# Silu as a tanh in one token chunk, the ends of the paired layers reordered, the first keys loaded in two pieces, and due times shifted from kept random seeds

## The chip, the cores and the metric

The kernel runs on one core of a Trainium2 chip. The metric is device time in microseconds of one execution. A core has a matrix engine (TensorE, PE in the profile, with PEld for its weight loads), a vector engine (VectorE, DVE), an engine for activation functions (ScalarE, ACT), GpSimd (POOL) and SyncE (SP), which issues nearly all DMAs here. Matrix products end in PSUM, of which the kernel uses eight banks of 128 x 512 fp32 numbers; all else lies in SBUF.

## The reference

```python
def phi(x):                        # x: 4 batches x 8 heads x 576 tokens x 64
    proj = einsum('bhsd,md->bhsm', x, omega)            # 128 features
    h = proj - sum(x * x, -1) / 2
    return exp(h - max(h, -1)) / sqrt(m)
q_p, k_p = phi(q * scale), phi(k * scale)
kv, z = k_p^T v, sum(k_p over tokens)
x = (q_p kv) / (q_p z + 1e-6)      # -> 2304 tokens x 512
g = x @ w_gate; x = (g * sigmoid(g) * (x @ w_val)) @ w_out     # 512 -> 1536 -> 512
out = ((x @ w_a) * (x @ w_b)) @ w_out2                          # 512 -> 1536 -> 512
```

## The kernel before

The 2304 tokens are cut into five chunks (`spans`): 512, 512, 256, 512 and 512 columns, features on the partitions. The first three go through attention and two feed-forward layers by `layer(c, m)`, with c the chunk and m = 0 for the layer with silu, 1 for the second. In it, each of 12 blocks `f` takes two PSUM banks, one for the gate and one for the value, of 4 x 3 products each (every fp32 product is made of three in fp32r: high x high, high x low, low x high; ACT makes the high part by a copy, DVE the low part by a subtraction, `wh`/`wl` for weights, `hh`/`hl` for the block's result). ACT applies Silu to the gate bank into `a` (L954), DVE multiplies it by the value bank into `h` (L957). A bank is free again when its last reader has ended. The last two chunks of 512 go together, by `pair(m)`, which makes 2 x 2 blocks in seven products in place of eight (`seven`, products p1 to p7 of mixed operands a11, s1 to s4, t1 to t4 and so on, each of 6 matmuls). `mixes` makes the activations' mixed operands ahead of a layer, `blocks` those of the inner result, `up` runs the first half, `down` and `plain` the second. `snap` copies a bank by ACT at its first use, `plus` adds one by DVE.

Attention of later chunks runs beside the layers of earlier ones. It needs Exp on ACT (L632), whose table set is another than that of Silu: between the two stands an ACT_TABLE_LOAD, which the compiler puts in.

The order of the instructions on each engine is made by a planner, `Plan`, when the program is built. Each step is recorded with its engine, an estimated duration, what it reads and writes, and a due time; `Plan.order` replays the steps on five engines and takes on each, whenever it comes free, the ready step with the earliest due time. It also deals out the buffers of each ring (PSUM banks among them) in that replay. The result is a fixed order for each engine. At run time an engine takes its instructions strictly in that order.

```python
on(ACT, act(n, 0, True), due, lambda a=a, ps=ps: nc.scalar.activation(
    out=a.tile[:, 0:n], in_=ps[0].tile[:, 0:n], func=AF.Silu if m == 0 else AF.Copy),
    reads=[(ps[0],)], writes=[(a,)], table="silu" if m == 0 else None)
on(DVE, dve(n), due, lambda a=a, h=h, ps=ps: nc.vector.tensor_tensor(
    out=h.tile[:, 0:n], in0=a.tile[:, 0:n], in1=ps[1].tile[:, 0:n], op=ALU.mult),
    reads=[(a,), (ps[1],)], writes=[(h,)])
```

Of the kernel before, what the change touches and what calls it, by code (L numbers as in the profile page):

```python
# [12 lines left out]
AF = mybir.ActivationFunctionType  # L13
# [3 lines left out]
P = 128  # L17
# [79 lines left out]
class Plan:  # L97
# [14 lines left out]
    RATE = 0.24  # L112
    HELD = {DVE: (1.0, 0.05), POOL: (1.0, 0.12)}
# [4 lines left out]
    def add(self, eng, pace, due, fn, reads=(), writes=(), lat=None, table=None, size=0.0, slack=0.0,  # L118
# [22 lines left out]
        return o  # L141

# [121 lines left out]
    def issue(self):  # L264
        for o in self.order():
            o.fn()
# [3 lines left out]
def attention_moe_moe(ctx: ExitStack, tc: tile.TileContext, qT, kT, q, k, v, omegaT,  # L270
# [217 lines left out]
    AHEAD = 20.0  # L488

# [43 lines left out]
    def features(rT, tok, nt, step, f, due, length, how, psum, first):  # L533
# [39 lines left out]
        for g in range(0, nt, size):  # L573
# [25 lines left out]
            else:  # L599
                ps = psum.buf()  # L600
                for i in range(n):
                    def proj(i=i, ps=ps, g=g):
# [8 lines left out]
                    on(PE, pe(0.36 if how == SPLIT else 0.45), d, proj,  # L611
                       reads=[(hi,), (lo,), (bdh,), (bdl,)] if how == SPLIT else
                       [(rT, *rT.state), (bd, *bd.state)], writes=[(ps, i)])
# [24 lines left out]
    def loads(rT, src, p, due, pieces):  # L638

        for b, a, z, to in pieces:  # L640
            on(SP, dma((z - a) / 2), due - 9, lambda b=b, a=a, z=z, to=to: nc.sync.dma_start(
                out=rT.tile[:, to:to + z - a], in_=src[b, p][:, a:z]), writes=[(rT, b)])
# [3 lines left out]
    def keys(b, p, due, length, how):  # L646

        rT, tok, vt = r_xT.buf(), r_kt.buf(), r_vt.buf()
        loads(rT, kT, p, due, [(b, 0, S, 0)])
# [9 lines left out]
                 first=due < 4)  # L659
# [265 lines left out]
    def layer(c, m):  # L925
# [16 lines left out]
        for f in range(NF):  # L942
# [4 lines left out]
            for g in range(2):  # L947
# [6 lines left out]
            on(ACT, act(n, 0, True), due, lambda a=a, ps=ps: nc.scalar.activation(  # L954
                out=a.tile[:, 0:n], in_=ps[0].tile[:, 0:n], func=AF.Silu if m == 0 else AF.Copy),
                reads=[(ps[0],)], writes=[(a,)], table="silu" if m == 0 else None)
            on(DVE, dve(n), due, lambda a=a, h=h, ps=ps: nc.vector.tensor_tensor(  # L957
                out=h.tile[:, 0:n], in0=a.tile[:, 0:n], in1=ps[1].tile[:, 0:n], op=ALU.mult),
                reads=[(a,), (ps[1],)], writes=[(h,)])
# [59 lines left out]
    def mixes(m, due, eng):  # L1019
# [6 lines left out]
        def keep(name, k, b):  # L1026
# [61 lines left out]
    def pair(m, eng):  # L1088
# [23 lines left out]
        def seven(w, x, late, read):  # L1112


            b0, b1, b2 = (ps_m.buf() for _ in range(3))
            b4, b3 = (b2, b1) if late else (b1, b2)
# [5 lines left out]
            for i, name in enumerate(order):  # L1122
                b, wn, xn, first, last = steps[name]
                product(b, w[wn], x[xn], now(6 * i), first, last)
                read(name, b)

        def up(f, late):
# [18 lines left out]
            seven(w, x, late, read)  # L1146
# [9 lines left out]
        def down(g, d, hx):  # L1156

            w = mixed_weights(m, 2 * NF + ND * d + g, 2 * NF + ND * (d + KD // 2) + g, now(), d == 0)
            e = now(42) - 15
# [5 lines left out]
            seven(w, hx, d == 0, read)  # L1165

        def plain(g, d, hx, more):
# [4 lines left out]
            for t, names in ((1, ("a21", "a22")), (0, ("a11", "a12"))):  # L1172
                for x, o in zip(i, (d, d + KD // 2)):
                    b = ps_m.buf()
                    hi, lo = parts_of[c, m, x]
                    for k, name in enumerate(names):
                        product(b, [(hi, lo, slice((2 * k + e) * P, (2 * k + e + 1) * P))
                                    for e in range(2)], hx[name], now(more), k == 0, k == 1)
                        more += 6
                    gain(b, (t, o), now(more) - 15)  # L1180
# [43 lines left out]
        for f, out in steps:  # L1224
# [90 lines left out]
```

## Time and profile before

| | us |
|---|---|
| median of 3 runs | 1002.58 (1001.65 to 1002.89) |
| profiled execution, its own time | 1005.29 |
| its span, first to last instruction | 1003.5 |
| PE busy in the span | 984.2 (98%) |
| DVE busy | 894.3 (89%) |
| ACT busy | 725.3 (72%) |
| POOL busy | 258.2 (26%) |

The profiled execution is 1.8 us longer than its span and 2.7 us longer than the median of the runs without a profile. Times below are from the span's start. PE is busy nearly always, so time can only be had where it waits, where its clock is low, or before its first and after its last matmul. The first chunk's attention stands alone in the first 57 us; the layers of the three single chunks go on to about 650 us (the third chunk's first layer from 529 to 575 us), the paired layers from 650 us to the end, with the step from the first to the second paired layer at 824 us.

### The profile page before, as it was taken

The page shows a single profiled execution, that of the slowest core. Times are in us where ns is not written, and L with a number is a line of the kernel's source. Part 1 is how long each engine was busy: PE and PEld are TensorE (multiplying, and loading weights), DVE is VectorE, ACT ScalarE, POOL GpSimd, SP SyncE. Part 2 cuts the span into 40 slices and gives each one's busy share as a digit, 9 for nine tenths or more (in the row PEclk, how much of TensorE's full clock was granted, in tenths as well). Part 3 has the DMA queues.
Part 4 walks back from the last instruction along what each step waited for, and adds up shares of the span by engine and source line. Part 5 has one row for each costly group of instructions (what it writes and reads, how often), then busy time and mean ns, then how long its engine had stood idle before and what let it go on. Part 6 is the DMA issues. An engine that isn't in the chain of part 4 may idle for free.

```text
span 1003.5 us, 15362 instructions
## 1 busy us (share of the span) xinstructions
PE 984.2 (98%) x5144; PEld 829.3 (83%) x5144; DVE 894.3 (89%) x1593; ACT 725.3 (72%) x1523; POOL 258.2 (26%) x207
## 2 busy tenths in 40 slices
PE   7999999999999999999999999999999999999998
PEld 6878888878878888888888999988888887888886
DVE  5999889999968889998978879989889788989997
ACT  5978878798789898879868978666574645556351
POOL 1220023413502333454356424112020021202020
PEclk9999999999999999999999999999999999999999
DMA  8778776686876567665654555511212301121212
GB/s 250 238 258 243 229 244 200 217 252 189 286 227 197 176 190 241 203 188 166 192 165 131 147 160 172 171 61 33 74 43 63 95 22 53 32 74 42 61 35 84
DMA packets 92400, 153.12 MB, mean 153 GB/s; under 512 B 8736, under 2 KB 41120, under 8 KB 92320
## 3 DMA queue, kind: packets, MB, share of 16 engines
q1 hardware_dynamic: 92240, 152.11, 49.3%
q8 instruction: 40, 0.66, 0.3%
q14 instruction: 40, 0.33, 0.1%
q10 hardware_dynamic: 80, 0.03, 0.0%
HBM read 128.52 MB, written 23.59 MB: 152 GB/s over the span
## 4 chain that ended last, share of the span: by engine, by line
PE 78%; DVE 9%; ACT 6%; DMA 3%; issue 2%; POOL 1%; SPq 0%; DVEq 0%; ACTq 0%; POOLq 0%
PE ps_m L994 12%; PE ps_m L936 12%; PE ps_m L937 11%; PE ps_m L938 11%; PE ps_t L994 8%; PE ps_p L994 8%; PE ps_kv L994 4%; PE ps_kv L663 3%; PE ps_p L583 2%; DMA w64a<-w 1%; PE ps_t L869 1%; DVE wl L478 1%; PE ps_p L609 1%; PE ps_t L854 1%; DVE w L905 1%
## 5 line engine op out<-in xcount | busy, mean ns | idle before, releaser
L478 DVE TENSOR_TENSOR wl<-w,wh 128x512 fp32r<-128x512 f32 x254 | 190.8, 761 | 10.2 <-ACT wh L917 9.6
L936 PE MATMUL ps_m<-xh,wh 128*128 128x512 f32 (+1 forms) x504 | 189.2, 375 | 3.2 <-ACT a L954 2.5
L937 PE MATMUL ps_m<-xl,wh 128*128 128x512 f32 (+1 forms) x504 | 184.7, 366 | 0.7 <-DVE xl L478 0.7
L938 PE MATMUL ps_m<-xh,wl 128*128 128x512 f32 (+1 forms) x504 | 184.5, 366 | 0.7 <-DVE wl L478 0.7
L917 ACT ACTIVATE wh<-w 128x512 fp32r<-128x512 f32 x220 | 135.9, 632 | 32.1 <-DVE w L905 18.6
L478 POOL TENSOR_TENSOR rs<-xT,rs 64x576 fp32r<-64x576 f32 (+4 forms) x48 | 67.9, 1414 | 201.4 <-ACT rs L566 114.6
L936 PEld LDWEIGHTS ps_m<-xh,wh 128*128 128x128 f32 x504 | 95.9, 190 | 18.2 <-ACT a L954 3.8
L938 PEld LDWEIGHTS ps_m<-xh,wl 128*128 128x128 f32 x504 | 95.6, 190 | 16.8 <-DVE wl L478 1.2
L937 PEld LDWEIGHTS ps_m<-xl,wh 128*128 128x128 f32 x504 | 95.9, 190 | 13.7 <-DVE xl L478 1.3
L936 PE MATMUL ps_m<-hh,wh 128*128 128x512 f32 (+1 forms) x240 | 90.9, 379 | 0.0
L937 PE MATMUL ps_m<-hl,wh 128*128 128x512 f32 (+1 forms) x240 | 88.6, 369 | 0.0
L938 PE MATMUL ps_m<-hh,wl 128*128 128x512 f32 (+1 forms) x240 | 88.6, 369 | 0.0
L905 DVE SCALAR_TENSOR_TENSOR w<-w,w64a 128x512 uint32<-128x512 uint32 x90 | 69.9, 780 | 5.3 <-ACT w L896 5.2
L902 DVE SCALAR_TENSOR_TENSOR w64a<-w64a 128x512 uint32<-128x512 uint32 x90 | 69.0, 772 | 3.0 <-ACT w64a L899 2.9
L899 ACT ACTIVATE w64a<-w64a 128x512 uint32<-128x512 uint32 x90 | 60.9, 681 | 13.4 <-DMA w64a<-w 12.9
L896 ACT ACTIVATE w<-w64a 128x512 f32<-128x512 f32 x90 | 60.1, 675 | 0.6 <-DVE wl L478 0.6
L478 DVE TENSOR_TENSOR hl<-h,hh 128x512 fp32r<-128x512 f32 (+1 forms) x72 | 51.9, 722 | 1.6 <-ACT hh L960 1.4
L938 PEld LDWEIGHTS ps_m<-hh,wl 128*128 128x128 f32 x240 | 45.2, 189 | 8.0
L936 PEld LDWEIGHTS ps_m<-hh,wh 128*128 128x128 f32 x240 | 45.3, 189 | 7.6 <-issue 1.7
L960 ACT ACTIVATE hh<-h 128x512 fp32r<-128x512 f32 (+1 forms) x72 | 40.3, 561 | 15.3 <-DVE h L957 15.1
L937 PEld LDWEIGHTS ps_m<-hl,wh 128*128 128x128 f32 x240 | 45.4, 189 | 5.9
L825 POOL TENSOR_TENSOR xt<-qf,fT 128x512 f32<-128x512 f32 (+2 forms) x31 | 35.3, 1140 | 49.9 <-ACT qf L632 26.7
(850 smaller groups left out, 2635.4 us busy)
## 6 DMA issues: line engine op xcount, KB each, us to landing
w64a<-w SPq DMA_DIRECT2D x90, 512.0 KB, 4.3
w<-kept SPq DMA_DIRECT2D x180, 256.0 KB, 2.7
kept<-w SPq DMA_DIRECT2D x72, 256.0 KB, 5.0
w64b<-w SPq DMA_DIRECT2D x18, 512.0 KB, 4.7
kt<-k_t SPq DMA_DIRECT2D x16, 320.0 KB, 3.8
vt<-v_t SPq DMA_DIRECT2D x16, 320.0 KB, 4.4
xT<-kT SPq DMA_DIRECT2D x16, 288.0 KB, 3.8
qt<-q_t SPq DMA_DIRECT2D x16, 256.0 KB, 4.0
```

The source lines that it names most:

```text
L478: eng.tensor_tensor(out=out, in0=a, in1=hi.bitcast(F32), op=ALU.subtract)
L825: nc.gpsimd.tensor_tensor(out=pr.tile.rearrange("p (t h m) -> p t h m", t=2, h=2)[lo_:hi_, i:i + m], in0=f.tile[lo_:hi_, g + i:g + i + m], ...
L896: on(ACT, act(CW + 50), due - ahead - 10, lambda: nc.scalar.activation(out=w.tile, in_=raw.tile[:, :, 1].bitcast(F32), func=AF.Abs, scale= ...
L899: on(ACT, act(CW + 50), due - ahead - 10, lambda: nc.scalar.activation(out=raw.tile[:, :, 0], in_=raw.tile[:, :, 0], func=AF.Copy, scale=0 ...
L902: on(DVE, dve(CW, True), due - ahead - 9, lambda: nc.vector.scalar_tensor_tensor(out=raw.tile[:, :, 0], in0=raw.tile[:, :, 1], scalar=0x80 ...
L905: on(DVE, dve(CW, True), due - ahead - 9, lambda: nc.vector.scalar_tensor_tensor(out=w.tile.bitcast(U32), in0=w.tile.bitcast(U32), scalar= ...
L917: on(ACT, act(CW), due - ahead - 7, lambda: nc.scalar.activation(out=hi.tile.rearrange("p a c -> p (a c)"), in_=w.tile, func=AF.Copy), rea ...
L936: nc.tensor.matmul(o, lhsT=hi.tile[:, wi], rhs=a, start=first, stop=False)
L937: nc.tensor.matmul(o, lhsT=hi.tile[:, wi], rhs=b, start=False, stop=False)
L938: nc.tensor.matmul(o, lhsT=lo.tile[:, wi], rhs=a, start=False, stop=last)
L960: on(ACT, act(n), due + 2, lambda h=h, hh=hh: nc.scalar.activation(out=hh.tile[:, 0:n], in_=h.tile[:, 0:n], func=AF.Copy), reads=[(h,)], w ...
L994: nc.tensor.matmul(ps.tile, lhsT=flat(a.tile)[:, k], rhs=b.tile, start=first and i == j == 0, stop=last and i == len(w) - 1 and j == 2, sk ...
```

## The change

Six edits, all in one diff:

- In the third chunk only (`TANH = (2,)`), silu of the gate bank is made from tanh: ACT takes tanh(g/2) into `a`, DVE makes a = (a + 1) * g from the gate bank, and then h = 0.5 * a * value in place of a * value. The step no longer asks for Silu's table set.
- `Plan.shift` adds to the due times, before the order is made, the random shifts of 16 fixed seeds.
- The first keys' transposed load is cut into two DMAs of 240 and 336 columns, and a projection waits for those of them that it reads.
- `seven` takes its PSUM banks as its products come and can be run in turns with another; in the second paired layer the last two `down` blocks run interleaved, after the first two products of each.
- The last `plain` block of the first paired layer makes its four outputs in another order.
- In `mixes` the operands a11 and s3 are due 6 us earlier; the cold first projections are recorded with a longer duration.

```diff
+    KEPT = (400000, 400001, 400011, 400014, 400026, 400048, 400059, 400114, 400140, 400491,
...
+    def shift(self):
+        for k in self.KEPT:
+            rnd = random.Random(k)
+            size, share = (0.5, 1.0, 2.0)[k % 3], (0.03, 0.1, 0.3)[k // 3 % 3]
+            for o in self.ops:
+                x = rnd.gauss(0, size) if rnd.random() < share else 0.0
+                if o.due > -1e5:
+                    o.due += x
...
-        loads(rT, kT, p, due, [(b, 0, S, 0)])
+        part = TS + P
+        loads(rT, kT, p, due, [(b, 0, part, 0), (b, part, S, part)] if due < 4 else [(b, 0, S, 0)])
...
+            how = AF.Copy if m else AF.Tanh if c in TANH else AF.Silu
+            half = 0.5 if how == AF.Tanh else 1.0
...
+            if how == AF.Tanh:
+                on(DVE, dve(n), due, lambda a=a, ps=ps: nc.vector.scalar_tensor_tensor(
+                    out=a.tile[:, 0:n], in0=a.tile[:, 0:n], scalar=1.0, in1=ps[0].tile[:, 0:n],
+                    op0=ALU.add, op1=ALU.mult), reads=[(ps[0],)], writes=[(a,)])
+                on(DVE, dve(n), due, lambda a=a, h=h, ps=ps: nc.vector.scalar_tensor_tensor(
+                    out=h.tile[:, 0:n], in0=a.tile[:, 0:n], scalar=0.5, in1=ps[1].tile[:, 0:n],
+                    op0=ALU.mult, op1=ALU.mult), reads=[(a,), (ps[1],)], writes=[(h,)])
...
-            keep("a11", k, x[0, k])
+            keep("a11", k, x[0, k], due - 6)
...
-            combine(eng[k], of(x[0, k]), of(x[1, k]), of(s3), ALU.subtract, due)
-            keep("s3", k, s3)
+            combine(eng[k], of(x[0, k]), of(x[1, k]), of(s3), ALU.subtract, due - 6)
+            keep("s3", k, s3, due - 6)
...
+        def run(*steps):
+            for x in steps:
+                next(x)
+                next(x)
+            for _ in zip(*steps):
+                pass
...
+            places = [(t, j) for t in (1, 0) for j in range(2)]
+            if d == KD // 2 - 1:
+                places = [(0, 0), (1, 0), (1, 1), (0, 1)]
...
-            else:
-                down(*out, hx[out[0]])
+            elif out[0] < ND - 1:
+                run(down(*out, hx[out[0]], out[1] == 0))
                 done += n_down // (KD // 2)
+            elif out[1] == 0:
+                run(*(down(*out[:1], d, hx[-1], True, lambda i, d=d: (
+                    i + 2 * d if i < 2 else 2 * i + d)) for d in range(KD // 2)))
+                done += n_down
```

The number of matmuls of each shape is the same in both programs. DVE has 12 instructions more, SP one DMA more, and ACT 14 table loads in place of 22: none of the six around the third chunk, and two fewer around the second.

Third chunk, ACT, around the copy that ends the first part of the fourth chunk's attention (L700, L720 after the change; line numbers past the diff are higher). Before:

```order
L960 ACTIVATE hh2_137<-h1_133 128x256
L917 ACTIVATE wh5_172<-w322_165 128x512
L700 ACTIVATE w64a_0__4811<-ps_t1_67 128x512
L954 ACT_TABLE_LOAD
L954 ACTIVATE a1_131<-ps_kv0_68 128x256
L954 ACTIVATE a0_130<-ps_m0_61 128x256
L592 ACTIVATE qf1_107<-ps_p0_64 128x256
```

After the change, ACT at the same place:

```order
L991 ACTIVATE hh3_138<-h2_134 128x256
L937 ACTIVATE wh5_172<-w320_163 128x512
L720 ACTIVATE w64a_0__4803<-ps_t0_66 128x512
L976 ACTIVATE a1_131<-ps_kv0_68 128x256
L937 ACTIVATE wh6_173<-w321_164 128x512
L991 ACTIVATE hh4_139<-h0_132 128x256
L610 ACTIVATE qf1_107<-ps_p0_64 128x256
```

L976 is the new tanh: it stands where a load and two Silus stood, and one more block has gone through by then.

The same chunk on DVE, at the second block's `h0` (den, rec and bias belong to attention). Before:

```order
L478 TENSOR_TENSOR wl5_179<-w320_163,wh5_172 128x512
L619 TENSOR_REDUCE bias0_92<-qf0_106 128x8
L957 TENSOR_TENSOR h0_132<-a1_131,ps_m0_61 128x256
L622 SCALAR_TENSOR_TENSOR bias0_92<-s0_89,bias0_92 128x8
L478 TENSOR_TENSOR wl6_180<-w323_166,wh6_173 128x512
```

After the change, DVE at the same place:

```order
L638 TENSOR_REDUCE bias0_92<-qf0_106 128x8
L852 TENSOR_REDUCE den1_99<-xt0_113 128x4
L981 SCALAR_TENSOR_TENSOR a1_131<-a1_131,ps_kv0_68 128x256
L856 TENSOR_SCALAR den1_99<-den1_99 128x4
L641 SCALAR_TENSOR_TENSOR bias0_92<-s0_89,bias0_92 128x8
L984 SCALAR_TENSOR_TENSOR h0_132<-a1_131,ps_m0_61 128x256
```

The gate bank `ps_kv0` is now let go by a DVE step (L981), and two small steps of attention stand between it and the one that lets go of the value bank.

The step from the first to the second paired layer, PE, third product of the new layer (its second k block is `xh5`, `xl5`) and what follows. Before:

```order
L994 MATMUL ps_p0_64<-kf0__5373,wl3_177 128x512
L994 MATMUL ps_p0_64<-xh5_119,wh3_170 128x512
L994 MATMUL ps_p0_64<-xl5_127,wh3_170 128x512
L994 MATMUL ps_p0_64<-xh5_119,wl3_177 128x512
L994 MATMUL ps_p1_65<-xT0__5932,wh6_173 128x512
L994 MATMUL ps_p1_65<-xT2__5977,wh6_173 128x512
```

After the change, PE at the same place:

```order
L1025 MATMUL ps_kv0_68<-kf0__5367,wl3_177 128x512
L1025 MATMUL ps_kv0_68<-xh5_119,wh3_170 128x512
L1025 MATMUL ps_kv0_68<-xl5_127,wh3_170 128x512
L1025 MATMUL ps_kv0_68<-xh5_119,wl3_177 128x512
L1025 MATMUL ps_m0_61<-kt0__4387,wh1_168 128x512
L1025 MATMUL ps_m0_61<-vt0__4646,wh1_168 128x512
```

The fourth product was the second one into the bank `ps_p1` of the same block; now it is the first product of the next block, into a bank of its own, and the one into `ps_p1` comes after it.

## Rows read from the trace of the kernel before

**Rows 1.** The page: span, and PE's busy time, share and instructions.

```profile
span 1003.5 us, 15362 instructions
PE 984.2 (98%) x5144; PEld 829.3 (83%) x5144; DVE 894.3 (89%) x1593; ACT 725.3 (72%) x1523; POOL 258.2 (26%) x207
```

**Rows 2.** Waits of PE: waited for, us in total, times, longest.

```profile
PE ps_m L936 <- ACT a L954: 2.5, 3, 1.1
PE ps_kv L936 <- ACT a L954: 1.8, 1, 1.8
```

**Rows 3.** Stretches: us, busy us of PE, PEld, DVE, ACT, POOL; granted clock, DMA share, GB/s.

```profile
0.00:57.00 57.00, 49.38 (x297) 41.78 (x298) 43.59 (x124) 42.56 (x119) 11.75 (x20) 1.00 0.81 252
57.00:502.00 445.00, 442.11 (x2229) 366.10 (x2228) 405.58 (x683) 377.22 (x805) 139.41 (x113) 1.00 0.70 215
531.70:575.70 44.00, 41.09 (x322) 39.07 (x321) 40.16 (x78) 39.44 (x90) 21.39 (x16) 0.96 0.46 135
```

**Rows 4.** Timeline of PE in the third chunk: start, us, what, idle before.

```profile
547.32 0.39 PE L936 MATMUL ps_kv<-xh,wh 128*128 128x256 f32 x1 [1.84 <-ACT a L954]
567.59 0.39 PE L936 MATMUL ps_m<-xh,wh 128*128 128x256 f32 x1 [1.07 <-ACT a L954]
```

**Rows 5.** Timeline of ACT at the first of these two.

```profile
545.58 1.28 ACT L954 ACT_TABLE_LOAD   x1
546.88 0.39 ACT L954 ACTIVATE a<-ps_kv 128x256 f32<-128x256 f32 x1
```

**Rows 6.** Stretches behind the first wait; third column from the right: granted clock.

```profile
549.00:550.00 1.00, 1.00 (x7) 1.00 (x6) 1.00 (x4) 1.00 (x3) 0.33 (x1) 0.50 0.72 229
...
552.00:555.00 3.00, 3.00 (x27) 3.00 (x26) 1.67 (x4) 2.60 (x7) 0.00 (x0) 0.96 0.68 216
```

**Rows 7.** Groups of DVE, 531.7 to 575.7 us: busy us, mean ns, idle before.

```profile
L478 DVE TENSOR_TENSOR wl<-w,wh 128x512 fp32r<-128x512 f32 x23 | 17.3, 763 | 0.0
...
L957 DVE TENSOR_TENSOR h<-a,ps_m 128x256 f32<-128x256 f32 x10 | 4.0, 407 | 0.6 <-PE ps_m L938 0.6
L836 DVE TENSOR_SCALAR den<-den 128x4 f32<-128x4 f32 x5 | 3.5, 700 | 0.0
...
L832 DVE TENSOR_REDUCE den<-xt 128x4 f32<-128x512 f32 x5 | 3.4, 675 | 3.8 <-POOL xt L825 3.8
L619 DVE TENSOR_REDUCE bias<-qf 128x8 f32<-128x1024 f32 x2 | 2.4, 1208 | 0.0
```

**Rows 8.** Timeline of DVE in the first chunk's attention: the same small step.

```profile
18.78 0.13 DVE L777 TENSOR_SCALAR den<-ps_t 128x4 f32<-128x4 f32 x1
```

**Rows 9.** Chain of waits in order of time: start, us, what; 30 undisturbed matmuls.

```profile
661.24 6.80 PE ps_m L994 x30
```

**Rows 10.** Timeline of PE at the start of the second paired layer.

```profile
827.45 0.39 PE L994 MATMUL ps_p<-kf__5373,wl 128*128 128x512 f32 x1
...
828.70 0.50 PE L994 MATMUL ps_p<-xl,wh 128*128 128x512 f32 x1 [0.23 <-DVE xl L478]
...
830.01 0.50 PE L994 MATMUL ps_p<-xT__5932,wh 128*128 128x512 f32 x1 [0.58 <-ACT ft__6043 L1100]
830.35 0.40 PE L994 MATMUL ps_p<-xT__5977,wh 128*128 128x512 f32 x1
```

**Rows 11.** Timeline of PE where the last `down` blocks begin.

```profile
983.54 0.50 PE L994 MATMUL ps_m<-hh,wh 128*128 128x512 f32 x1
984.92 0.50 PE L994 MATMUL ps_m<-hh,wh 128*128 128x512 f32 x1 [0.88 <-DVE hh L478]
```

**Rows 12.** Timeline of the first 12 us: DVE's scaling of the projection, PE.

```profile
3.93 0.29 DVE L512 TENSOR_SCALAR bd<-bd 128x256 f32<-128x256 f32 x1 [2.58 <-DMA bd<-omegaT]
4.65 4.60 PE L609 MATMUL ps_m<-bd,xT 128*128 128x256 f32 x10 [4.65 <-DMA xT<-kT]
9.42 2.04 PE L609 MATMUL ps_p<-bd,xT 128*128 128x256 f32 x8 [0.16 <-DMA xT<-qT]
```

**Rows 13.** Timeline of the end: PE's last matmul.

```profile
999.03 0.39 PE L994 MATMUL ps_kv<-hh,oms__6396 128*128 128x512 f32 x1
```

More of the change, by code (lines that the diff above doesn't have):

```diff
@@ L1 @@
 import heapq
+import random
 from contextlib import ExitStack
@@ L264, in issue @@
     def issue(self):
+        self.shift()
         for o in self.order():
@@ L530, in constants, with features @@
                     reads=[(x,)], writes=[(oms, (i, h))], after=ALONE)
-    def features(rT, tok, nt, step, f, due, length, how, psum, first):
+    def features(rT, tok, nt, step, f, due, length, how, psum, first, cold=False):
         width = step * (nt - 1) + P
@@ L953, in layer @@
             h_of.append((hh, hl))
[L954 to L959, printed above, removed]
+            how = AF.Copy if m else AF.Tanh if c in TANH else AF.Silu
+            half = 0.5 if how == AF.Tanh else 1.0
+            on(ACT, act(n, 0, True), due, lambda a=a, ps=ps, how=how, half=half: nc.scalar.activation(
+                out=a.tile[:, 0:n], in_=ps[0].tile[:, 0:n], func=how, scale=half),
+                reads=[(ps[0],)], writes=[(a,)],
+                table="silu" if how == AF.Silu else None)
+            if how == AF.Tanh:
[5 more added lines that the diff above has]
+                    op0=ALU.mult, op1=ALU.mult), reads=[(a,), (ps[1],)], writes=[(h,)])
+            else:
+                on(DVE, dve(n), due, lambda a=a, h=h, ps=ps: nc.vector.tensor_tensor(
+                    out=h.tile[:, 0:n], in0=a.tile[:, 0:n], in1=ps[1].tile[:, 0:n], op=ALU.mult),
+                    reads=[(a,), (ps[1],)], writes=[(h,)])
             on(ACT, act(n), due + 2, lambda h=h, hh=hh: nc.scalar.activation(
@@ L1110, in gate, with seven @@
                     out=u.tile, in_=u.tile, func=AF.Silu), writes=[(u,)], table="silu")
-        def seven(w, x, late, read):
-            b0, b1, b2 = (ps_m.buf() for _ in range(3))
-            b4, b3 = (b2, b1) if late else (b1, b2)
+        def seven(w, x, late, read, turn=lambda i: i):
+            banks = {}
+            b0, b4, b3 = range(3)
             steps = {"p1": (b0, "b11", "a11", True, False), "p2": (b4, "b21", "a12", True, True),
@@ L1123, in seven @@
                 b, wn, xn, first, last = steps[name]
-                product(b, w[wn], x[xn], now(6 * i), first, last)
-                read(name, b)
+                if first:
+                    banks[b] = ps_m.buf()
+                product(banks[b], w[wn], x[xn], now(6 * turn(i)), first, last)
+                read(name, banks[b])
+                yield
+        def run(*steps):
[4 more added lines that the diff above has]
+                pass
         def up(f, late):
@@ L1164, in read @@
                     gain(b, (t, d + i * KD // 2), e)
-            seven(w, hx, d == 0, read)
+            return seven(w, hx, late, read, turn)
         def plain(g, d, hx, more):
@@ L1171, in plain @@
                 weights(c, m, x, now(more))
[L1172 to L1180, printed above, removed]
+            places = [(t, j) for t in (1, 0) for j in range(2)]
+            if d == KD // 2 - 1:
+                places = [(0, 0), (1, 0), (1, 1), (0, 1)]
+            for t, j in places:
+                b = ps_m.buf()
+                hi, lo = parts_of[c, m, i[j]]
+                for k, name in enumerate(("a21", "a22") if t else ("a11", "a12")):
+                    product(b, [(hi, lo, slice((2 * k + e) * P, (2 * k + e + 1) * P))
+                                for e in range(2)], hx[name], now(more), k == 0, k == 1)
+                    more += 6
+                gain(b, (t, d + j * KD // 2), now(more) - 15)
         hx, rows_of = [{} for _ in range(ND)], [[] for _ in range(ND)]
```

25 lines of the change are left out of this document (16 added, 9 removed).

## The prediction

> **What bounds the kernel now.** The page comes first: PE is busy for 984.2 of 1003.5 us [rows 1]. The change leaves the number of matmuls as it is, so it can win only what PE spends waiting, at a low clock, or outside its work. The list of PE's waits then says who keeps it: the largest that a reordering can reach are waits for ACT's `a`, the silu, which lets go of a PSUM bank, 2.5 us in three and 1.8 us in one [rows 2]. The stretches say where: of the first 57 us PE is idle for 57 - 49.38 = 7.6, of the 445 us after them for 2.9, and of the 44 us of the third chunk's first layer for 44 - 41.09 = 2.9 [rows 3]. In that last stretch the granted clock is 0.96, in the others it is 1.00. So the reader looks there first.
>
> There the timeline shows PE waiting 1.84 us at 547.3 and 1.07 us at 567.6, both for `a` [rows 4], and ACT beginning a table load just before, at 545.58, with the Silu that PE needs 1.30 us behind it [rows 5]. Behind the first wait the clock is at 0.50, the lower level of 1.2 GHz, for the three slices from 549 to 552 (the first is shown), and at 0.96 in the next three us [rows 6]. In the paired layers PE has two disturbances, at 827 and 984 us [rows 10, 11]. The end is fixed: from the start of the last matmul at 999.03 to the end of the span are 4.4 us [rows 1, 13], for the last bank's addition and its store, which stay.
>
> **The third chunk.** No table load stands there any more. What that can give back at most is the idle time, 2.9 us, and the half clock: 3 x 0.5 + 3 x 0.04 = 1.6 us of lost matmul time [rows 6]. PE's need in the stretch falls from 44.0 to 39.5 us.
>
> A load and the gap behind it cost 1.30 us here [rows 5]. The Trainium skill ("ScalarE: Activation LUTs", What ACT_TABLE_LOAD costs) gives about 2.66 us for a switch, a drain behind the load included, which this trace does not show. With that figure the four loads of the stretch would weigh 10.6 us on ACT instead of 5.2, yet the gain would still be capped by the idle time that PE has, so the ceiling stays.
>
> Against it stand twelve more DVE steps, (a + 1) * g, one a block. No such step is in the trace; the nearest is `h`, of the same size and with one operand in PSUM, at 407 ns [rows 7], so 12 x 0.407 = 4.9 us. From the first block's `h` to the last block's, DVE also has one more maximum (1.2), one more sum (0.7) and one more addition of attention (about the 0.4 of an `h`), and two subtractions fewer (2 x 0.76): +0.8. DVE was busy for 40.16 of the 44 us [rows 3]; it would now need 45.9, which is more than PE's 39.5. The engine with the most work there changes.
>
> Two things soften that. A part of the 40.16 us is waiting within an instruction: the step on 4 numbers a partition takes 700 ns in this stretch, with POOL at work beside it, and 130 ns in the first chunk [rows 7, 8]; for five of them that is 2.9 us, and what waits there is no work, so 43.0 remain. And DVE's weight splits, 22 between the two ends in both orders, may be some steps ahead of PE when the stretch begins. The bounds: if every new step falls where DVE waited, PE sets the time and the stretch gives 4.5 us; if none does, it takes 45.9 and loses 1.9. I take 42.0, the 43.0 less about one and a third splits of lead: **-2.0**. It lies between the two ends because no row says how many waits are filled.
>
> The row of 700 ns against 130 speaks for a port that DVE shares with POOL. The Trainium skill ("SBUF — State Buffer", Who interferes with whom) says that a pair of ports is held by one of the two for a whole instruction, and that a DVE instruction with two SBUF inputs is locked out while GpSimd reads. By this rule the new steps, with one input in PSUM, never wait; their price would be the 0.407 us without surcharge, as the sum already has it.
>
> **From the first to the second paired layer.** Undisturbed, a matmul of 512 columns follows the one before after 6.80 / 30 = 0.227 us [rows 9]. From 827.45 to 830.35 there are five steps (one matmul in each of two gaps between the rows is not shown), so 1.13 us were due and 2.90 passed: 1.77 lost [rows 10]. The first 0.8 of it is the wait for the second half of operand s2. Its last ingredient came from the third output of the last `plain` block, followed by two subtractions, s3 and then s2. In the new order of outputs s3 is made after the second one, so a single subtraction is left when the third comes; a DVE step of 512 columns is some 0.76 us [rows 7], about what is missing. The next 0.9 is the wait for the snapshot that clears the bank's turn at 830.01; in its place stands the next block's first product, six matmuls or 1.36 us, which covers it, if its weights are split by then. If the cover fails, the whole 1.77 stays. Bounds -1.8 and 0; I take **-1.4**, as both waits are shorter than what is put before them.
>
> **The last blocks.** At 984.92 PE waits in the second product for the low part of the last operand: 1.38 us for a step of 0.227, so 1.15 lost [rows 11]. Now the first two products of both blocks come ahead, two more than before, or 2.7 us of cover. Bounds -1.15 and 0, taken **-1.1**. The interleaving moves the banks' additions closer together, but the tail of 4.4 us begins at the last of them in either order.
>
> **The start.** PE waits for the first keys until 4.65, while the scaled projection `bd` is ready at 3.93 + 0.29 = 4.22 [rows 12]: at most -0.4 for the smaller first DMA. The extra issue moves every later load back on SP, and the first queries' load now stands behind their token-major copy, 256 KB more at 252 GB/s [rows 3], so 1.0 us; PE waited for it at 9.42 [rows 12], and the first gather is queued behind it on PE. Bounds -0.4 and +1.0, taken 0.
>
> **The second chunk and the shifts.** Two of its twelve table loads go; of the 2.5 us of waits for `a`, 1.07 is the third chunk's, so 1.4 is here [rows 2, 4]. Two in twelve is -0.2; I take **-0.3**, between -1.4 and 0, since not every load had a wait behind it. All other orders change too. What they can win is the idle time left, 7.6 - 4.65 = 3.0 before 57 us and 2.9 after [rows 3, 12], and hardly more than half of it; what they can lose is a new wait such as the one at 547 us with its clock, 1.84 + 1.6 = 3.4. Bounds -3.0 and +3.4, taken 0, since the rows favour neither.
>
> **The sum.** -2.0 - 1.4 - 1.1 + 0 - 0.3 = -4.8 us. The span goes from 1003.5 to 998.7, the profiled execution from 1005.29 to 1000.5. The median of the runs stands 2.7 us below that execution, so from 1002.58 to **997.8 us**.
>
> **Rivals.**
> - *DVE takes over in the third chunk.* For: 45.9 us of demand against 39.5, and den and bias steps of attention between the two steps that let go of a block's banks. Against: at least 2.9 us of it is waiting. With none of the waits filled the term is +1.9 in place of -2.0: -0.9 in all, 1001.7, no measurable change.
> - *The same, with the clock: slower than before.* Where DVE is late at each of the twelve blocks, PE waits again and again for a bank, and after a wait of 1.84 us the clock fell for about three us, at 1.6 us [rows 4, 6]. Three such falls and the +1.9 make +6.7 for the stretch, less 2.8 of the other terms: +3.9, 1006.5. It decides from the point where the stretch takes more than 44 + 2.8 + 2.0 = 48.8 us. Against: its longest wait had a 1.3 us load behind it, which is gone.
> - *A shift opens a wait elsewhere*, of the size of the one at 547 us: -4.8 + 3.4, 1001.2.
> - *The paired layers' reordering doesn't bite*, because the late operand has moved with its consumers: both waits stay, -2.3, 1000.3.
> - *Everything fits*: every new DVE step in a wait, both waits of the paired layers gone, a few of the others too: -4.5 - 1.8 - 1.15 - 2 = -9.4, 993.1.
>
> **Chances.** The forecast as it stands, with one or the other term half filled (995 to 1000.5): 0.50, in it the reordering that doesn't bite. Everything fits: 0.15. DVE takes over: 0.15. A wait opened elsewhere: 0.10, most of it still faster. Slower by the clock: 0.10. A measurement of this kernel tells some 0.2%, 2 us, from no change. Faster by more than that, below 1000.6: 0.50 + 0.15 + 0.07 = 0.72; the same: 0.15 + 0.03 = 0.18; slower: 0.10. The range leaves out the slower rival and the tail of the best one: 993.0 to 1002.5.
>
> **What the profile would show.** No table load and no wait of PE for `a` between 530 and 575 us, granted clock 1.00 there, and the stretch from the first block's `h` to the last's in 40 to 43 us with DVE nearly without idle time. PE's starts 0.227 us apart at the beginning of the second paired layer and in the last two blocks. The first matmul at about 4.3 us. The forecast is wrong if PE waits in the third chunk for DVE's L981 or L984, if any slice shows a clock below 1.00 before the end, or if the idle time of PE before 502 us grows by more than 2 us.

## The result, and the profile after

The changed kernel takes 993.38 us (median of four runs, 992.62 to 995.26) against 1002.74 us for the kernel before (four runs, 1001.65 to 1003.07). The medians differ by 9.4 us; the ratio is 0.9915 with a 95% interval of 0.9900 to 0.9929, so 7.1 to 10.0 us of 1002.7. The forecast was 997.8 us in a range from 993.0 to 1002.5: right in direction, 4.4 us short in size. The time is that of the rival "everything fits" (993.1). Of its terms the third chunk's came out and the paired layers gave more than theirs; a gain elsewhere is not shown.

The page of the changed kernel, whose profiled execution took 995.26 us, for [rows 1]:

```profile
span 993.4 us, 15333 instructions
PE 979.6 (99%) x5144; PEld 827.1 (83%) x5144; DVE 889.7 (90%) x1605; ACT 711.6 (72%) x1515; POOL 264.2 (27%) x207
```

The span is 10.1 us shorter; PE is busy 4.6 us less for the same matmuls, and idle 5.5 us less. Its largest waits, for [rows 2] (us in total, times, longest):

```profile
PE ps_m L627 <- DVE bd L530: 3.8, 1, 3.8
PE ps_m L956 <- ACT a L976: 1.3, 1, 1.3
PE ps_t L760 <- ACT qf L651: 0.9, 1, 0.9
PE ps_p L627 <- DMA xT<-qT: 0.8, 1, 0.8
```

One wait for `a` is left of four. It is in the second chunk, where Silu still is. No wait for the new DVE steps, L981 and L984, is in the list. The stretches, for [rows 3], the third being the one between the third chunk's first and last `h`, the fourth the paired layers:

```profile
0.00:57.00 57.00, 49.30 (x297) 41.72 (x298) 44.15 (x123) 41.85 (x118) 11.28 (x20) 1.00 0.76 253
57.00:502.00 445.00, 442.66 (x2237) 366.88 (x2236) 401.93 (x684) 374.95 (x806) 144.85 (x113) 1.00 0.68 215
...
531.46:573.54 42.08, 42.08 (x347) 40.17 (x347) 41.39 (x89) 34.17 (x84) 23.75 (x18) 1.00 0.42 132
644.00:989.70 345.70, 345.66 (x1526) 285.89 (x1524) 315.06 (x559) 188.81 (x340) 43.48 (x29) 1.00 0.19 56
```

The first 57 us have as much idle time as before (7.7 us). In the third chunk PE is busy throughout at clock 1.00, and DVE for 41.39 of 42.08 us: both are full, where before PE stood idle for 2.9 us.

To see where the 10 us of the span went, four of PE's starts are compared: the first matmul of the third chunk's first layer, the last of that layer's first half, the first of the paired layers, and the last of all. Timeline of PE before (the last one is [rows 13]):

```profile
527.88 0.28 PE L936 MATMUL ps_m<-xh,wh 128*128 128x256 f32 x1
...
574.42 0.28 PE L936 MATMUL ps_m<-xh,wh 128*128 128x256 f32 x1
...
650.16 0.40 PE L994 MATMUL ps_m<-kt__4402,wh 128*128 128x512 f32 x1
```

And after:

```profile
526.71 0.28 PE L956 MATMUL ps_m<-xh,wh 128*128 128x256 f32 x1
...
568.58 0.28 PE L956 MATMUL ps_m<-xh,wh 128*128 128x256 f32 x1
...
644.03 0.40 PE L1025 MATMUL ps_kv<-kt__4387,wh 128*128 128x512 f32 x1
...
989.27 0.39 PE L1025 MATMUL ps_t<-hl,oms__6387 128*128 128x512 f32 x1
```

From the first to the second start 46.54 us became 41.87 (**-4.7**). Up to the first it is -1.2, from the second to the third -0.3, from the third to the fourth (348.87, now 345.24) **-3.6**, and behind it -0.3. The same for all profiled executions, as times of start and lengths in us:

| program | third chunk begins | its first half | paired layers | span |
|---|---|---|---|---|
| before | 527.88 | 46.54 | 348.87 | 1003.5 |
| after | 526.71 | 41.87 | 345.24 | 993.4 |
| tanh alone | 525.16 | 41.91 | 349.17 | 996.6 |
| ends alone | 525.55 | 44.98 | 345.41 | 996.1 |
| keys in two pieces alone | 527.21 | 48.04 | 349.18 | 1004.6 |
| shifts alone | 534.56 | 48.08 | 351.24 | 1012.6 |
| Silu in the changed order | 528.73 | 43.76 | 345.24 | 999.9 |
| last DVE step doubled | 525.43 | 43.71 | 345.24 | 995.1 |
| no shift | 529.16 | 45.37 | 345.89 | 1000.7 |
| no shift, early step | 528.79 | 41.72 | 345.44 | 996.3 |
| other seeds | 524.91 | 44.06 | 347.11 | 996.4 |
| third seeds | 528.38 | 48.21 | 348.75 | 1004.8 |
| tanh, ends, early step | 526.02 | 42.74 | 345.65 | 994.4 |
| after, early step | 525.68 | 42.60 | 345.24 | 993.1 |

Three things limit what the table can tell. "After", "Silu in the changed order", "last DVE step doubled" and "after, early step" have the same instructions in the same order up to 525 us, and yet begin the third chunk between 525.43 and 528.73. "Before", "tanh alone", "ends alone" and "tanh, ends, early step" share their order up to there too, and begin it between 525.16 and 527.88. So differences of two or three us in the first column come without any edit, and the -1.2 in it is not shown to be a gain.

The two next columns, which are measured from start to start, are steadier, but a fall of the clock enters them: "ends alone" has the order of the kernel before through the whole third chunk and took 44.98 us there at clock 1.00, where "before", with the fall of [rows 6], took 46.54. So of the -4.7 about 1.6 is the clock, and the 3.1 left are for the most part PE's waits (1.84 and 1.07).

The fall is not in every execution. For each run the mean granted clock is on record. Of the 42 runs of the kernel before that were made beside the experiments, 23 have 0.997 or 0.998 and a median of 1003.4 us, and 19 have 0.999 or 1.000 and a median of 1001.6. All four runs of the changed kernel have 0.999 or 1.000.

### The profile page after: what moved, and what is told of

The parts are those of the page before. It is cut to its first block, busy times and chain, and to the rows that moved or that the text cites. A ratio compares the mean times of both kernels' runs of the same rounds, so it can differ in the third digit from the quotient of the medians.

```text
span 993.4 us, 15333 instructions
## 1 busy us (share of the span) xinstructions
PE 979.6 (99%) x5144; PEld 827.1 (83%) x5144; DVE 889.7 (90%) x1605; ACT 711.6 (72%) x1515; POOL 264.2 (27%) x207
## 4 chain that ended last, share of the span: by engine, by line
PE 49%; DVE 7%; ACT 2%; POOL 2%; DMA 1%; issue 1%; SPq 0%; DVEq 0%; POOLq 0%
PE ps_m L1025 12%; PE ps_t L1025 9%; PE ps_p L1025 9%; PE ps_kv L1025 5%; PE ps_m L956 3%; PE ps_m L958 3%; PE ps_m L957 3%; DVE wl L495 1%; POOL xt L845 1%; ACT kf L651 1%; DVE w64a L922 1%; DVE w L925 1%; DVE bias L638 1%; PE ps_kv L956 1%; PE ps_kv L958 1%
## 5 line engine op out<-in xcount | busy, mean ns | idle before, releaser
L956 PE MATMUL ps_m<-hh,wh 128*128 128x512 f32 (+1 forms) x264 | 97.2, 368 | 0.0
L958 PE MATMUL ps_m<-hh,wl 128*128 128x512 f32 (+1 forms) x264 | 95.4, 361 | 0.0
L957 PE MATMUL ps_m<-hl,wh 128*128 128x512 f32 (+1 forms) x264 | 95.4, 361 | 0.0
L925 DVE SCALAR_TENSOR_TENSOR w<-w,w64a 128x512 uint32<-128x512 uint32 x90 | 66.5, 742 | 6.7 <-ACT w L916 6.2
L958 PEld LDWEIGHTS ps_m<-hh,wl 128*128 128x128 f32 x264 | 49.9, 189 | 7.9
L956 PEld LDWEIGHTS ps_m<-hh,wh 128*128 128x128 f32 x264 | 49.9, 189 | 7.2 <-issue 1.0
L957 PEld LDWEIGHTS ps_m<-hl,wh 128*128 128x128 f32 x264 | 49.9, 189 | 6.1
```

The costliest lines, as they stand in the source:

```text
L925: on(DVE, dve(CW, True), due - ahead - 9, lambda: nc.vector.scalar_tensor_tensor(out=w.tile.bitcast(U32), in0=w.tile.bitcast(U32), scalar= ...
L956: nc.tensor.matmul(o, lhsT=hi.tile[:, wi], rhs=a, start=first, stop=False)
L957: nc.tensor.matmul(o, lhsT=hi.tile[:, wi], rhs=b, start=False, stop=False)
L958: nc.tensor.matmul(o, lhsT=lo.tile[:, wi], rhs=a, start=False, stop=last)
```

## The experiments

The theory: the third chunk's gain comes from `a` being ready in time without table loads, and the new DVE work costs PE nothing as long as PE has other work at hand. The main rival: the gain comes from the new order and the shifts, whatever function ACT computes. For the rest, the reordered ends stand against the view that the shifts did it. Ratios are to runs of the kernel before made beside each, so two versions are compared by their ratios rather than by their medians.

**Tanh alone**, on the kernel before.

```diff
+    TANH = (2,)
+            how = AF.Copy if m else AF.Tanh if c in TANH else AF.Silu
```

> The kernel before with tanh in the third chunk as the only edit. Theory A (the loads made the loss): 3 to 5 us faster than before, 997.5 to 999.5, clock 1.00 in the third chunk. Theory C, that DVE's added steps take back half of it, as the prediction had it: 2 us faster, 1000 to 1001.5, with PE waiting for DVE between 530 and 580 us.

Measured: 997.91 us, ratio 0.9956 (0.9945 to 0.9968), by which -4.4 us (so for all that follow). The stretch of the third chunk is 41.91 us, as in the changed kernel, and the waits of the paired layers [rows 10, 11] are still there. All five runs have a mean clock of 0.999 or 1.000. So this part gives its whole gain without any of the others.

**Silu in the changed order.** The order of the changed kernel is kept, and ACT takes Silu of g/2 in place of tanh, so the layer computes another function; the compiler puts six table loads back.

```diff
-                out=a.tile[:, 0:n], in_=ps[0].tile[:, 0:n], func=how, scale=half),
+                func=AF.Silu if how == AF.Tanh else how, scale=half),
```

> The changed kernel with every instruction in its place, but ACT applies Silu instead of Tanh in the third chunk (so what that chunk's first layer computes is another function); the compiler puts back six table loads there, the two added DVE steps stay. Theory A, that the loads alone made the waits and the half clock of the third chunk: about 3 to 5 us slower than the changed kernel, 996.5 to 998.5, with PE waiting there for ACT or for DVE's steps behind ACT, and a clock of 0.5 for some us if one wait is as long as 1.8 us. Theory B, that the other order of attention in that stretch took the waits away: not over 1 us slower, 993 to 994.5.

Measured: 999.7 us, ratio 0.9969 (0.9959 to 0.9980), by the ratios 5.4 us more than the changed kernel; theory A had 3 to 5. Timeline of ACT, and of PE behind it:

```profile
563.09 1.28 ACT L976 ACT_TABLE_LOAD   x1
564.39 0.38 ACT L976 ACTIVATE a<-ps_m 128x256 f32<-128x256 f32 x1
```

```profile
565.28 0.39 PE L956 MATMUL ps_m<-xh,wh 128*128 128x256 f32 x1 [1.08 <-DVE a L982]
```

The wait is put down to DVE's step, but that step stands behind the late `a`, which began 1.30 us after its load, as in [rows 5]. The stretch is 1.9 us longer than in the changed kernel, the 76 us behind it 2.6 (78.03 against 75.45), the paired layers equal. Of the 6.5 us by which this span is longer, 4.5 thus stand where the programs differ, by the function and its loads; the other 2.0 stand before the third chunk, where they don't. No fall of the clock is needed for it: nine of the eleven runs have 0.999 or 1.000. The rival falls: the order without the tanh has no clean third chunk.

**The last DVE step doubled**, in the order of the changed kernel: h is computed twice in each block of the third chunk.

```diff
+                    for _ in range(2):
+                        nc.vector.scalar_tensor_tensor(out=h.tile[:, 0:n], ...)
```

> The changed kernel in its own order, with the last DVE step of each block of the third chunk done twice (the same result), 12 x 0.41 = 4.9 us more of DVE work there. Theory E, DVE at its limit, so that the twelve steps of the change were paid by chance of placement alone: 3 to 6 us slower than the changed kernel, 996.5 to 999.5, PE waiting for DVE between 530 and 580 us. Theory F, that PE has other work at hand while DVE lags: not over 1.5 us slower, up to 995.

Measured: 996.85 us, ratio 0.9936 (0.9921 to 0.9950), by the ratios 2.1 us more than the changed kernel, hardly beyond the uncertainty of the two, for 12 x 0.41 = 4.9 us of DVE work. Timeline of PE:

```profile
555.12 0.38 PE L956 MATMUL ps_m<-xh,wh 128*128 128x256 f32 x1 [0.88 <-DVE a L981]
...
573.08 0.39 PE L958 MATMUL ps_m<-hh,wl 128*128 128x256 f32 x1 [0.60 <-DVE wl L495]
```

The stretch grows by 1.8 us and the 75 us behind it by 1.1 (76.58 against 75.45). So 2.9 of the 4.9 us are paid for in this trace, as theory E has it and not F. The first extra step brought no wait of PE over 0.2 us in the third chunk of the changed kernel, this one three: the changed kernel stands near the edge of what DVE can take there.

**The paired ends alone**: the orders of `plain`, `down` and `mixes`, as in the change, and nothing else.

```diff
+            places = [(t, j) for t in (1, 0) for j in range(2)]
+            if d == KD // 2 - 1:
+                places = [(0, 0), (1, 0), (1, 1), (0, 1)]
```

> The kernel before with the paired layers' edits alone (outputs of the last plain block reordered, a11 and s3 due earlier, the last two blocks interleaved). Theory A: PE's waits at about 827 and 984 us gone, 2.5 to 3.3 us faster than before, 999.5 to 1000.5. Theory G, that the late operand has only moved: within 1 us of before.

Measured: 999.9 us, ratio 0.9969 (0.9958 to 0.9980), -3.1 us; the paired layers shrink by 3.5 us, and both their waits are gone. The third chunk's wait stays. Timeline of PE, and the stretch behind it:

```profile
544.98 0.39 PE L936 MATMUL ps_kv<-xh,wh 128*128 128x256 f32 x1 [1.84 <-ACT a L954]
```

```profile
546.00:549.00 3.00, 3.00 (x28) 3.00 (x27) 3.00 (x8) 2.21 (x6) 0.97 (x1) 1.00 0.44 100
```

The wait is as long as in [rows 4], but here the granted clock stays at 1.00 behind it, where in [rows 6] it was 0.50. The eight runs fall into two groups, 997.2 and 997.9 us against six from 999.3 to 1000.5; the two have a mean clock of 1.000 and 0.999, the six of 0.997 or 0.998. So the same order runs with the fall and without it, and most of its runs have it.

**No shift.** The changed kernel without the call of `Plan.shift`.

```diff
-        self.shift()
```

> The changed kernel without the shifts of due times; all else as changed. Theory A, that the shifts only shuffle (zero on the mean, as the prediction took them) and tanh, paired ends and the first loads make the gain: 992 to 996. Theory B, that the kept shifts are what removes PE's waits, and the other edits alone leave waits of the old kind: 998 to 1003, with PE's waits spread over the first 500 us or in the paired layers.

Measured: 999.25 us, ratio 0.9966 (0.9954 to 0.9978). So without the shifts the rest of the change is worth 3.4 us, no more than the tanh alone. PE waits 3.3 us in four waits for Silu's `a` in the chunks before the third (1.3 in one in the changed kernel), and once in the third chunk. Timeline of ACT, DVE and PE there, and the stretch behind:

```profile
539.71 0.36 ACT L975 ACTIVATE a<-ps_m 128x256 f32<-128x256 f32 x1
```

```profile
539.70 1.24 DVE L855 TENSOR_SCALAR den<-den 128x4 f32<-128x4 f32 x1
540.85 0.68 DVE L494 TENSOR_TENSOR wl<-w,wh 128x512 fp32r<-128x512 f32 x1
541.45 0.16 DVE L858 RECIPROCAL rec<-den 128x4 f32<-128x4 f32 x1
541.54 0.65 DVE L851 TENSOR_REDUCE den<-xt 128x4 f32<-128x512 f32 x1
542.11 0.73 DVE L980 SCALAR_TENSOR_TENSOR a<-a,ps_m 128x256 f32<-128x256 f32 x2
```

```profile
542.57 0.44 PE L955 MATMUL ps_m<-xh,wh 128*128 128x256 f32 x1 [2.26 <-DVE a L980]
```

```profile
543.00:546.00 3.00, 3.00 (x17) 3.00 (x15) 3.00 (x9) 1.65 (x4) 1.33 (x1) 0.50 0.47 145
```

The tanh was ready at 540.07. The step that lets go of the bank stood behind four others in DVE's queue, three of them for attention, and began at 542.11. PE waited 2.26 us, and the clock was at 0.50 for the three us behind. This is the rival "DVE takes over, with the clock", once instead of three times. The fall is not what keeps this kernel's time up: this profiled execution took 1002.45 us, the five runs with a mean clock of 1.000 have the median of all, 999.25.

**No shift, early step.** To test that reading: the same, with the first new DVE step due 4 us earlier.

```diff
-                on(DVE, dve(n), due, lambda a=a, ps=ps: nc.vector.scalar_tensor_tensor(
+                on(DVE, dve(n), due - 4, lambda a=a, ps=ps: nc.vector.scalar_tensor_tensor(
```

> The kernel without shifts, with the first added DVE step, (a + 1) * g, due 4 us earlier, so that at the place of the long wait (542 us) it stands right behind the small den step and not behind a weight split and a sum as well. Theory D, that it is the place of this one step in DVE's queue, and the half clock that a long wait brings, that cost the kernel without shifts its gain: the wait goes from 2.3 to about 1.0 us, no half clock there, 2.5 to 3.5 us faster than without shifts, 995.5 to 997. Theory E, that DVE has too much work in the third chunk (busy for 41.4 of 42.1 us there in the changed kernel): the wait turns up at another block, 998.5 to 1000.

Measured: 996.15 us, ratio 0.9941 (0.9927 to 0.9955), by the ratios 2.5 us less than without it. The stretch falls from 45.37 to 41.72 us, as theory D has it. The wait is cut and the clock does not fall behind it:

```profile
540.92 0.39 PE L955 MATMUL ps_m<-xh,wh 128*128 128x256 f32 x1 [0.99 <-DVE a L980]
```

One due time does in the third chunk what the sixteen seeds did.

**Other seeds.** Two sets of sixteen seeds that nobody had chosen, each seed raised by 9000, and by 18000.

```diff
-            rnd = random.Random(k)
+            rnd = random.Random(k + 9000)
```

> The changed kernel with sixteen other seeds, of the same sizes and shares, which nothing has selected. Theory A (the shifts only shuffle): 992 to 996, as without shifts. Theory B (selection among seeds is what counts): 997 to 1004, worse than the kept seeds by 4 us or more, as random shifts undo places that were right.

> The changed kernel with another sixteen seeds that nothing has selected. If shifts only shuffle, between the two that are known without selection, 997.2 and 999.3, give or take 2 us: 995 to 1001. If the kept seeds gain by having been selected, it stays above the changed kernel's 993.4 by 2 us or more.

Measured: 997.2 us, ratio 0.9945 (0.9933 to 0.9957), and 1005.76 us, ratio 1.0030 (1.0018 to 1.0041). The first set leaves a wait of 1.43 us in the third chunk, without a fall of the clock. The second, outside the 995 to 1001 that were expected, moved the first keys' load behind others, and then paid again in the third chunk (48.21 us) and in the paired layers (348.75 us). PE in the first set, then in the second:

```profile
559.26 0.38 PE L956 MATMUL ps_m<-xh,wh 128*128 128x256 f32 x1 [1.43 <-DVE a L981]
```

```profile
6.76 3.75 PE L627 MATMUL ps_m<-bd,xT 128*128 128x256 f32 x8 [6.76 <-DMA xT<-kT]
```

Unchosen shifts give 997.2 and 1005.8, none gives 999.3, the kept ones 993.4. By the ratios the two sets are 2.1 us better and 6.4 us worse than none, and the kept ones 5.1 better. Two sets show no worth of shifts as such; which one is kept decides on this list of steps.

**Keys in two pieces alone**, with the longer recorded duration of the cold projections.

```diff
+        part = TS + P
+        loads(rT, kT, p, due, [(b, 0, part, 0), (b, part, S, part)] if due < 4 else [(b, 0, S, 0)])
```

> The kernel before with the first keys' load in two pieces and the cold projections' longer duration, nothing else. Theory K0 (the earlier first matmul is given back before 57 us, as the changed kernel's trace shows): 1001.5 to 1003.8 us, PE's first matmul at 3.8 to 4.4 us, the first layer's first matmul within 0.5 us of 55 us. Rival K1 (it is worth its 0.8 us): 1000.5 to 1002 with the first layer's start 0.8 us earlier. Rival K2 (the longer duration in the planner's list reorders what comes after, and that opens or closes a wait): outside 1000.5 to 1004, with the place to be seen in the list of PE's waits.

Measured: 1006.39 us, ratio 1.0036 (1.0022 to 1.0050), slower by 3.6 us. The first matmul is at 3.80 us, yet the first layer starts at the same time as before within half a us. The loss is 500 us later, in the third chunk. ACT and PE there, and the stretch behind:

```profile
562.26 1.28 ACT L956 ACT_TABLE_LOAD   x1
563.56 0.38 ACT L956 ACTIVATE a<-ps_m 128x256 f32<-128x256 f32 x1
```

```profile
564.00 0.39 PE L938 MATMUL ps_m<-xh,wh 128*128 128x256 f32 x1 [3.72 <-ACT a L956]
```

```profile
566.00:568.00 2.00, 2.00 (x11) 2.00 (x11) 2.00 (x7) 0.93 (x3) 0.51 (x1) 0.50 0.64 190
```

Rival K2 holds: the edit changes the planner's replay from the first us, and one Silu of the third chunk falls behind a group of Exps and a load. So the loss shows in the order, not at the DMA; which of the two parts of the edit moves the order was not separated. All five runs have a mean clock of 0.998 or less, against four of the nine beside them, so a part of the loss is likely the fall, coming every time.

**The kept shifts alone**, on the kernel before.

```diff
+        self.shift()
         for o in self.order():
```

> The kernel before with the kept shifts alone. Theory F (the shifts fit the list that they were selected on and are as good as any other seeds on another): 998 to 1009 us, waits of PE over 1 us at places where the kernel before has none. Rival P (the kept shifts have a worth of their own, some 3 us): 998 to 1000.5 with fewer waits before 502 us than the 2.9 us of the kernel before.

Measured: 1015.63 us, ratio 1.0131 (1.0110 to 1.0152), slower by 13.1 us, worse than the range that was expected. Of its waits, two of PE's, and the stretches behind them:

```profile
555.13 0.38 PE L953 MATMUL ps_kv<-xh,wh 128*128 128x256 f32 x1 [2.53 <-ACT a L971]
...
990.91 0.79 PE L1011 MATMUL ps_kv<-hh,wh 128*128 128x512 f32 x1 [2.73 <-DVE w64a__5296 L1121]
```

```profile
555.20:561.00 5.80, 5.80 (x49) 5.80 (x50) 5.80 (x15) 5.34 (x14) 3.76 (x3) 1.00 0.53 149
991.00:994.00 3.00, 3.00 (x7) 2.38 (x8) 3.00 (x6) 0.88 (x2) 0.00 (x0) 0.51 0.00 0
```

The shifts that go with 993.4 us on one list go with 1015.6 on another. They have no worth of their own that goes with them to another list.

**Tanh, ends and the early step**, on the kernel before, without shifts and with the keys in one piece.

> The kernel before with tanh in the third chunk, the paired layers' reordered ends, and the first added DVE step due 4 us earlier; no shifts, keys in one piece. Theory A (the two parts add up, since they work 80 us and more apart): tanh alone gave -4.8 us and the ends alone -2.8 to -3.5, so 994.5 to 996 us, no wait in the third chunk over 1.1 us, paired layers without waits. Rival S (the shifts hold a gain of their own in the first two chunks that no other part gives): the time is the same, and 1.2 to 2 us of waits stay before 500 us that the changed kernel does not have. Rival I (the parts disturb each other through the planner): over 997 us.

Measured: 995.57 us, ratio 0.9928 (0.9914 to 0.9943), -7.2 us. Tanh alone and ends alone make -4.4 - 3.1 = -7.5, so the parts add up within the uncertainty. Rival S finds no support: before 502 us PE is idle for 9.5 us here and for 10.0 in the changed kernel.

**The changed kernel with the early step.**

> The changed kernel with the first added DVE step of each third-chunk block due 4 us earlier; the shifts are the kept ones. Theory F (the kept shifts fit one list of steps and were selected on it; any change of the list loses some of that): 994.5 to 998 us, with a wait that the changed kernel does not have. Rival G (the early step is worth its 3 us whatever else stands): 990 to 992.5. Rival N (the kept shifts already removed the wait that the early step removes): 992.5 to 994.5, the same as the changed kernel.

Measured: 994.86 us, ratio 0.9924 (0.9908 to 0.9940). Its interval overlaps with that of the changed kernel, so theories F and N can't be told apart; rival G is out, and the early step brings nothing where no wait is left for it. No version is below the changed kernel's ratio, and the one without shifts and split keys stands within 0.0013 of it, less than the two intervals leave open. The shifts and the split keys are thus not shown to add anything to tanh, ends and one early due time.

## Why the prediction was short

**The third chunk was the mis-sized term.** Forecast -2.0 us, measured -4.7 between PE's starts, about the ceiling of 4.5 that the prediction gave for PE: the idle time and the half clock both came back whole. The step that failed is the one that let DVE's stretch be PE's time: "I take 42.0 ... **-2.0**". The 42.0 us from the first `h` to the last came true, with 42.08. But the 44.0 us that it was taken from begin before the first `h` (533.01 to 576.12 makes 43.1), so by DVE's measure the stretch shrank by 1.0 us while PE gained 4.7. DVE's last `h` of this layer starts at 573.14, 4.56 us behind PE's last first-half matmul at 568.58. It, and PE's stretch between the two:

```profile
573.14 0.41 DVE L984 SCALAR_TENSOR_TENSOR h<-a,ps_m 128x256 f32<-128x256 f32 x1
```

```profile
568.58:573.14 4.56, 4.56 (x41) 4.56 (x40) 4.56 (x8) 2.24 (x4) 1.53 (x2) 1.00 0.31 102
```

Before, it lagged by 1.30 us (575.72 against 574.42). PE didn't wait for it: it is busy all the time between, in the second half's products of finished blocks (`hh`, `hl`) and in attention, and has no wait over 0.2 us in the rest of the layer. The lag grew by 3.3 us and cost nothing. The prediction had no term for work that PE has at hand while DVE lags. What DVE did in the stretch (busy us, mean ns), for [rows 7]:

```profile
L495 DVE TENSOR_TENSOR wl<-w,wh 128x512 fp32r<-128x512 f32 x22 | 15.3, 708 | 0.1
...
L984 DVE SCALAR_TENSOR_TENSOR h<-a,ps_m 128x256 f32<-128x256 f32 x12 | 4.9, 410 | 0.0
...
L981 DVE SCALAR_TENSOR_TENSOR a<-a,ps_kv 128x256 f32<-128x256 f32 x6 | 2.5, 412 | 0.3 <-ACT a L976 0.3
...
L856 DVE TENSOR_SCALAR den<-den 128x4 f32<-128x4 f32 x5 | 1.9, 380 | 0.0
```

The new steps take 0.41 us each, the price that was taken from `h`, and the rule of the Trainium skill ("SBUF — State Buffer", Who interferes with whom) that was quoted for them is not contradicted. The small `den` step took 380 ns in place of 700, so less was waited inside it. The 130 ns of [rows 8] are of another step, one that reads PSUM; the reading holds even so. Without shifts the step itself took 1.24 us once (539.70 above), to the end of a POOL instruction, and was part of PE's wait; 3 us later, between two POOL instructions, it took 0.15. POOL, then DVE:

```profile
539.60 1.32 POOL L844 TENSOR_TENSOR xt<-qf,fT 128x512 f32<-128x512 f32 x1 [0.86 <-DVE den L851]
```

```profile
542.77 0.15 DVE L855 TENSOR_SCALAR den<-den 128x4 f32<-128x4 f32 x1
```

That 42.0 was hit is in part luck: no run shows the lead of the weight splits by which 43.0 became 42.0, and DVE was busy for 41.39 us, not 43.0.

**The table loads** went as said. The Trainium skill's 2.66 us a switch ("ScalarE: Activation LUTs", What ACT_TABLE_LOAD costs) is again not what was measured: in the run with Silu in the changed order `a` began 1.30 us after the start of its load.

**The paired layers** gave 3.6 us (3.1 by the ratio of the run alone) where 1.4 + 1.1 = 2.5 were taken and 2.95 was the ceiling of the two places. Both waits are gone, with no shortfall of cover. Some 0.6 us more was not priced: the steps beside the wait at 984 us were long too (0.4 us in all), and so were two at 880 us (0.2 us). Which of the reordering's parts did what was not separated. The step to the second paired layer, for [rows 10]:

```profile
821.31 0.39 PE L1025 MATMUL ps_kv<-kf__5367,wl 128*128 128x512 f32 x1
821.54 0.39 PE L1025 MATMUL ps_kv<-xh,wh 128*128 128x512 f32 x1
821.76 0.39 PE L1025 MATMUL ps_kv<-xl,wh 128*128 128x512 f32 x1
821.99 0.39 PE L1025 MATMUL ps_kv<-xh,wl 128*128 128x512 f32 x1
822.22 0.39 PE L1025 MATMUL ps_m<-kt__4387,wh 128*128 128x512 f32 x1
```

The starts are 0.22 to 0.23 us apart, and no bracket with a wait stands behind any; so it goes on to the last blocks.

**The start** was right at 0, by another way than its bounds. The first matmul is at 3.82 us, more than the 0.4 allowed, because the scaling of `bd` also came earlier, and the queries' load took most of that back: its matmuls start at 9.26, before at 9.42. Timeline of PE and of DVE, for [rows 12]:

```profile
3.82 4.63 PE L627 MATMUL ps_m<-bd,xT 128*128 128x256 f32 x10 [3.82 <-DVE bd L530]
9.26 0.92 PE L627 MATMUL ps_p<-bd,xT 128*128 128x256 f32 x3 [0.80 <-DMA xT<-qT]
```

```profile
3.48 0.29 DVE L530 TENSOR_SCALAR bd<-bd 128x256 f32<-128x256 f32 x1 [2.13 <-DMA bd<-omegaT]
```

By 57 us nothing of it is left. What the part on the start missed is that this edit, with the longer recorded duration, changes the whole order behind it, by +3.6 us when made alone; the prediction had that risk only under the shifts.

**The second chunk and the shifts**: -0.3 taken, -1.2 seen up to the third chunk. Four executions of the old order begin that chunk at 525.2 to 527.9 and four of the new one at 525.4 to 528.7, so no gain is shown there. The bounds of the shifts, -3.0 and +3.4, were too narrow for shifts as such: one set of other seeds cost 6.4 us against none, and the kept ones 13.1 us on another list.

**The rivals.** DVE did become as full as the first one said; its price was not paid by PE. The second, with the clock, is seen at one block in the trace without shifts, but that kernel is still faster than before. The reordering did bite. No new wait over 0.2 us opened behind 502 us.

## What to carry to other kernels

In this kernel a full engine cost time only where its lateness held something that the leading engine needed next, most often a bank, and near that edge little more work fitted; ask which of its steps lets go of a bank, put that one early, and let the rest lag. A small edit under a planner is two edits, the step itself and a new order for everything after it; price the second one too, and measure it by making the edit alone. Due times found by search belong to the list of steps on which they were found: on another list the same seeds lost 13 us, and one reasoned due time, with tanh and ends, came as near to the changed kernel as the measurement can tell.

## What the runs showed of the hardware

After waits of PE of nearly one length the granted clock sometimes fell to 0.50 and sometimes did not. It fell behind 1.84 us in the kernel before [rows 4, 6], 2.26 us without shifts, 3.72 us with the keys alone, and, with the shifts alone, 2.73 us at the end and a pair of 1.61 and 0.41 us at 159 us. It stayed at 1.00 behind 1.84 us at the same instruction with the ends alone, 1.43 us with other seeds, and 2.53 and 2.28 us in the third chunk of the shifts alone. The length of the wait by itself does not decide it, and neither does the order: the kernel before fell in some 23 of 42 runs, by their mean clock, at 1.9 us between the medians. These runs don't show what does. So a wait that brings a fall in some executions should be priced with a share of it, and a single profile doesn't tell the share.

The other surprise is the 3.3 us by which executions of one order differ before the third chunk.
